# One core, LSH attention and a Mish feed-forward in one program: a new table of order and engine, and the bias of the exponential made by column

## The chip, the cores and the metric

The kernel runs on one core of a Trainium2 chip. The metric is the device time of one execution in microseconds. TensorE (PE) multiplies matrices, VectorE (DVE), ScalarE (ACT) and GpSimd (POOL) work on elements, and SyncE (SP) issues the DMAs.

## The reference, cut to what matters

```python
# q, k, v: (4, 8, 768, 64) float32;  proj: (64, 6);  w_in: (512, 2048);  w_out: (2048, 512)
q_bits = (einsum('bhsd,dk->bhsk', q, proj) > 0)      # 6 hash bits a token
k_bits = (einsum('bhsd,dk->bhsk', k, proj) > 0)
mask   = bucket(q_bits)[..., :, None] == bucket(k_bits)[..., None, :]
scores = where(mask, q @ k^T / 8, -1e9)
scores = scores - max(scores)
attn   = exp(scores) / (sum(exp(scores)) + 1e-9)
x      = (attn @ v), heads side by side              # (3072, 512)
h      = x @ w_in
out    = (h * tanh(softplus(h))) @ w_out             # (3072, 512)
```

The inputs are float32. The matmuls of the kernel run in float16, with every operand split into a high part and a rest.

## The kernel before, in words

The rows are worked through in 12 units of 256 tokens. A unit has 8 attention steps, each with the scores of two heads for 128 tokens, and 8 feed-forward steps, each with 256 columns of the inner width. Step numbers run through the program: S0 to S95 are the score matmuls (line 802), V0 to V47 the products with v (line 882, one for two score steps), H0 to H95 the first matmul of the feed-forward (lines 913 to 915), and O the second (lines 951 to 953, two for each H).

One attention step goes like this. PE fills `ps_s`, which exists once and holds the scores of both heads, with S. DVE takes the negated maximum of each head (line 809), makes from it a factor (line 812: the scale where the maximum is that of a real key, else 0) and a bias (line 815: maximum times factor); all of them lie in the small tile `svb`, one column for a head. ACT does the exponential of each head with this bias and factor (line 825) into `pb`, and sums it. Only then may the next S overwrite `ps_s`. The sums are inverted (lines 838, 841, 847). The attention is split into float16 parts in `hl`: the high part ("hi") on POOL, ACT or DVE (lines 365, 367, 368), the rest ("lo") in one instruction of DVE (line 386) or in two of POOL (lines 392 and 393). SP then transposes `hl` into `PT` by DMA (line 427), and V reads that. The lines 809 to 815 have two forms: one that treats the two heads' columns in one instruction (128x2), and one that takes each column by itself (128x1, twice).

In a feed-forward step ACT does Mish on the accumulators (line 931) and DVE, ACT and POOL split the result for O. Mish and the exponential need different tables of ACT, so an `ACT_TABLE_LOAD` stands wherever the one follows the other.

At the start the program also loads k, v, q and the weights, splits the weights (16 pieces, up to about step S16), and for the first keys and values makes the rests on PE (line 414). Keys and queries are transposed by DMA (`KT`, `QT`), hashed on PE (line 666), and the hash bits of both are written by DVE (line 674) and transposed as well; S0 needs all four.

What runs where, and in which order, is no decision of the code at run time. Every step of the program is an entry with one to four alternatives (an engine, a cost, a function). `ORDER` is a table of 2639 numbers, each with a letter for the alternative; the program issues the entries in the table's order, and each engine works through its own part in that order. SP issues all DMAs from one queue.

Of the kernel before, what the change touches and what calls it, by code (L numbers as in the profile page):

```python
# [92 lines left out]
151b 143 244b 141c 146c 317 76 144 147 152 153 159 107c 145 148 191c 184 160 183 108 149 218 245c 192 171 172
219 193 164b 194b 199 200 228 195 268b 201 227 162 226 202 173b 165 203b 185 197 204 211 174b 161 205 229 246
207b 212b 196 175 230 247 213 186 214 187 206b 220 296 231c 221 209 163 386 198 269b 208 232 222 239 240b 223
254 233 270b 235 92 189 255 234 241 210 236 224 242 256c 237 264 225 271 257 258c 238 272 297 265b 298b 260b 273
259b 274 281 176 266 188 276 267 280 262 284c 279 299 282 300 261 292 275 283 285 322b 263 248 287 277 348 286b
293b 249 288 333 294 290 190 295 289 349 307 309c 310 334 311 308 250b 350c 318 251b 312 335 319b 291 301 320
313b 252 302 351 321 304c 315 344 352 373b 303c 253 323b 336b 337 314 360 338 324 345 353 346 325 359 316 340
326 347 374 341 339c 354 305 327 375b 413 361b 328 362 306 342 376 356 369 398 355c 414 357 329b 343 363 330c  # L100
399 278 415b 370b 377 331 365b 400 364c 372 378 367 371 379 416 385 387 384 409 453b 381 401b 366 402 368 435
425 434 403b 388 404b 436 446 332 410b 454b 424 417 389b 380b 405 455c 412 411 391 382 456 447 479c 407 358 448
426b 449 406 427 480b 418 419 392 429b 408 393 450b 462 394 457 421 463 428b 383 430 420b 481b 422 432 451 482
437 431 458 390b 452 475 423 464b 483 459 514 433 465 489 466 460b 438 476 468 515 442 477 395 478 467c 469 396
439 516c 470 490c 517 507 443 599 488 491 440 508 509 492c 493 510 494b 484 485 499 518 444b 511b 486b 519 520
441 496 487 526c 397 461 445 512 527b 513 471 521b 535c 503 472 500 536 495 501 497 504 528b 547 523 548 537 473
522 505b 596 597 529 502 530 592 598 531 498 524 474 538 539 525 532 506 544 533c 550 534 540 551b 541 552 553c
549 561b 574c 554 582 560 600 555 556 601 557 575 543 588 558c 576 559 562 565c 566 542 602 563b 567b 564 568
569 578 577c 570 619 545 620 571 585 603 604c 589 615 572c 605 580 621 643 622 606c 623 579 573 581 616b 624
608b 593 714 546 625c 644 617 584 647 651 618 627 586 626b 658 628 587 583 594c 654 590c 634 591 652 609 595 645  # L110
689 612 635 607 653 715 716 718 636 659 688 610b 655b 660 613 661 656 638 629 662c 646 664 630 637 614 642 632
657 648 717 842 671c 631 611 639 665 640b 633 672 649b 684 673 679 674 685 650 675 719 677 663c 680 686 720c 687
703 722 641 690 681 666 704 726 667 691 692 682 705b 669 668 676 693 711 707b 738 727b 730 706 678 694b 729 696
670 697 739 741 728 753 712 721 742 709 723 695c 740 757 752 758 710 743b 731 734 732 759 760 754b 744 724c 708
698 745b 751 735 755 699 761 725 747 762 763c 780 756 765 772 746 788 773 700 733 701 749 736 748 783 766 781
774 791 789 784b 775 785 776 782 702 838 792 737 806 786 750 777 807 802 790 778 793c 794 892 803 795 787 834
833 804 797 805 846 825d 826 796c 779 835 764c 808 799 809 767 839 840b 850 800 768 810 827b 851 847b 821 836
837 854 811 845 769 812b 822 770 855 844 829 801 871 843 823 798 848 858 841 849 771 814 863c 873 828b 852c 813
853 859 864 872 815 831 865 867b 860 874b 893 816 817 886 894 895 713 1112 819 832 905 875 896c 876 830 877c 885
898 856b 888 866 868 899 818 857 878 820 906 869b 887 879 861b 889b 881 880b 907 890 891 870 908 919 911 1023  # L120
912 900 883b 922 913b 882 901 923b 915 941 914c 924 917 683 925 1068 909 926 884 927 942 897b 920 943 937 945
938 946 862 928 947 939 934 953 916 935b 918 949 930 944 948 970 929b 940 960b 1069 1111 968 931 954 961 932b
971 950 962b 903 1070 1071 824 964 963 933 951 972 973 969 983 966 982 957 952 965 985 974 955 975 976b 986 902
978 967 984 987 989 977c 979 1113 988 958 993 1015 956 1002 1001 904 994 1019 995c 980b 1016 1003 996c 959 1072b
1074 1028 1020 997 990 1004 1005 1017 999 1073c 1006b 1230 991 981 1075 1007 1021 1018 1260 1008b 1024 1025 1010
998 936 1026 1014 992 1048 1009c 1027 1012 1032 1022 1029 1049 1033 1039d 1040 1047 1061 1000 1041b 1030 1050b
1076 1043 1232 1034c 1051 1052 1011 1077 1013 1042b 1231 1062 1036 1031 1045 1053d 1054 1037 1233 1064 1035 910b
1038 1044 1063 921 1234 1055 1093 1065 1235 1081 1066 1082 1057 1067 1046 1056c 1085b 1083 1086 1059b 1087c 1084
1058 1096 1097 1098 1089 1088b 1099 1108 1094 1114 1100 1101 1118 1060 1115 1090 1078 1200 1102c 1119 1091 1122
1103 1123 1120c 1104 1106 1116b 1124 1125 1092 1137b 1117 1134 1135 1126 1138 1109 1121 1130 1147 1139b 1136  # L130
1145 1141b 1107 1148b 1105 1127 1131 1146 1079 1140b 1159 1149 1095 1132 1133 1150 1128c 1151b 1152 1129 1192
1142 1162 1193 1196 1153 1163b 1143b 1154b 1161 1157 1236b 1155 1194c 1293 1197 1080 1144 1178 1164 1165 1167
1170c 1179 1171 1168 1156 1160 1195 1224 1172 1205 1173b 1237 1180 1198b 1174 1181 1238 1182 1176b 1158 1201
1183b 1184 1185b 1166 1202b 1209 1169 1187b 1213 1203 1204 1199 1226 1216c 1175 1253 1177 1186b 1214 1206 1191
1217 1218c 1188 1189b 1227 1239 1207c 1292 1220 1210 1228 1225 1215 1190 1229 1208 1219 1254 1211c 1273 1240
1221 1212 1256 1245d 1241 1246 1261 1222 1110 1255 1247b 1257 1249 1258 1223 1259 1315 1248b 1274 1275 1251 1276
1277d 1288 1278 1279 1281b 1289b 1290 1262 1322 1263 1316b 1291 1318 1250 1326 1323 1285 1243 1280b 1319 1252
1320b 1264c 1282 1283 1307d 1308 1242 1324 1327 1330 1309 1321 1266 1328 1334 1331 1286b 1311 1310b 1313 1335
1338 1351 1332c 1284 1244 1325 1329 1353 1333 1343c 1339 1442 1267 1352 1312 1265 1294 1336 1344 1345b 1340 1381
1268 1354 1347 1387 1269 1295 1346b 1355 1337 1314 1356 1296 1380 1383 1297 1341c 1271 1349 1492 1287 1298b  # L140
1372d 1373 1348 1270 1350 1433 1374b 1384 1375 1376 1385 1386 1272 1382 1388 1378 1389 1377 1342 1300 1393c 1402
1358 1394 1395 1403 1299 1397 1391 1404 1434 1357 1301 1405 1438 1390 1396b 1446 1435 1392 1379 1439 1359 1302
1398 1450 1399 1360 1303 1425 1304 1305 1440b 1426 1427b 1306 1361 1447 1362 1451 1363b 1454 1436 1452b 1428c
# [950 lines left out]
```

## Time and profile before

| | before |
|---|---|
| median of 3 runs | 876.47 us (876.2 to 877.28) |
| profiled execution, span | 876.5 us |
| PE busy | 803.2 us (92%) |
| DVE busy | 695.7 us (79%) |
| ACT busy | 597.0 us (68%) |
| POOL busy | 280.6 us (32%) |
| ACT table loads | 74 |

The profiled execution's span, from the first to the last instruction, is its device time here; it equals the median of the runs. In the page, "busy" of an engine is the time in which it executes; a busy digit in the 40 slices is the tenth of a slice. PE's work comes in a fixed amount, so the time is PE's busy time and the time in which PE has nothing to do.

### The profile page before, as it was taken

How to read it: one execution, taken by the hardware profiler on the slowest of the kernel's cores; microseconds unless marked ns; L12 is line 12 of the kernel's file. 1: busy time of each engine (PE TensorE's matmuls, PEld its weight loads, DVE VectorE, ACT ScalarE, POOL GpSimd, SP SyncE). 2: the span in 40 equal slices, each digit the busy share in tenths (PEclk: the TensorE clock that was granted, in tenths of full speed). 3: DMA queues.
4: the chain of work that ended last, by engine and by line, in shares of the span. 5: the costliest groups of instructions: out<-in, count | busy, mean ns of one | idle time of the engine just before them, and what ended most of it. 6: DMA issues, size and time to landing. Idle time of an engine off the chain costs nothing.

```text
span 876.5 us, 17009 instructions
## 1 busy us (share of the span) xinstructions
PE 803.2 (92%) x6530; PEld 536.5 (61%) x6530; DVE 695.7 (79%) x1344; ACT 597.0 (68%) x947; POOL 280.6 (32%) x260
## 2 busy tenths in 40 slices
PE   2676679899999999999999999999999999999998
PEld 1343347566666767666656766666665766776665
DVE  4697999999899887788889879879888777676412
ACT  5587889878786667668777766567876756657411
POOL 4226443134146433443223212133413143351000
PEclk9697999999999999999999999999999999999999
DMA  9999989589999797688999966899997866556400
GB/s 279 268 243 235 215 195 224 155 187 196 200 172 173 146 186 123 132 156 169 211 188 192 175 122 117 150 178 182 230 161 143 154 120 129 101 98 128 78 25 25
DMA packets 432689, 143.73 MB, mean 164 GB/s; under 512 B 402912, under 2 KB 423392, under 8 KB 432608
## 3 DMA queue, kind: packets, MB, share of 16 engines
q1 hardware_dynamic: 432608, 142.65, 80.9%
q8 instruction: 51, 0.84, 0.4%
q14 instruction: 30, 0.25, 0.1%
HBM read 35.65 MB, written 6.29 MB: 48 GB/s over the span
## 4 chain that ended last, share of the span: by engine, by line
PE 58%; DVE 23%; DMA 8%; ACT 6%; issue 4%; SPq 1%; ACTq 0%; DVEq 0%
PE ps_s L802 10%; PE ps_t L882 8%; DVE svb L809 7%; PE ps_acc L913 7%; PE ps_o L951 6%; PE ps_acc L915 6%; PE ps_acc L914 6%; PE ps_o L953 6%; PE ps_o L952 6%; ACT pb L825 3%; DMA QT<-tok 3%; DVE hl L386 3%; DVE svb L812 1%; DVE ffb L386 1%; DVE svb L815 1%
## 5 line engine op out<-in xcount | busy, mean ns | idle before, releaser
L825 ACT ACTIVATE pb<-ps_s,svb 128x768 f32<-128x768 f32 x192 | 188.8, 986 | 100.9 <-DVE svb L815 84.5
L913 PE MATMUL ps_acc<-X,wi 128*128 128x256 f16 x768 | 209.8, 273 | 0.5 <-ACT ffb L931 0.5
L914 PE MATMUL ps_acc<-X,wi 128*128 128x256 f16 x768 | 209.6, 273 | 0.0
L915 PE MATMUL ps_acc<-X,wi 128*128 128x256 f16 x768 | 209.6, 273 | 0.0
L809 DVE TENSOR_REDUCE svb<-ps_s 128x2 f32<-128x1536 f32 x96 | 168.3, 1753 | 40.6 <-PE ps_s L802 39.4
L386 DVE SCALAR_TENSOR_TENSOR hl<-pb,svb,hl 128x768 f16<-128x768 f32 x146 | 155.8, 1075 | 3.3 <-POOL hl L365 2.7
L802 PE MATMUL ps_s<-KT,QT 128*128 128x512 f16 (+1 forms) x768 | 146.1, 335 | 10.3 <-ACT pb L825 9.7
L953 PE MATMUL ps_o<-wo,ffb 128*128 128x512 f16 x384 | 145.7, 379 | 0.3 <-DVE ffb L386 0.3
L951 PE MATMUL ps_o<-wo,ffb 128*128 128x512 f16 x384 | 145.7, 379 | 0.0
L952 PE MATMUL ps_o<-wo,ffb 128*128 128x512 f16 x384 | 145.7, 379 | 0.0
L365 POOL TENSOR_SCALAR hl<-pb,svb 128x768 f16<-128x768 f32 x66 | 65.3, 990 | 169.8 <-DVE svb L847 73.2
L882 PE MATMUL ps_t<-PT,VT 128*64 128x256 f16 x1728 | 107.6, 280 | 10.9 <-DVE hw L456 4.2
L802 PEld LDWEIGHTS <-QT 128*128 128x128 f16 x768 | 74.2, 99 | 67.2 <-issue 24.1
L882 PEld LDWEIGHTS <-VT 128*64 128x64 f16 x1728 | 94.5, 113 | 29.4 <-issue 23.8
L931 ACT ACTIVATE ffb<-ps_acc,smalls 128x512 f32<-128x512 f32 x96 | 63.5, 684 | 56.0 <-PE ps_acc L915 51.6
L367 ACT ACTIVATE hl<-pb,svb 128x768 f16<-128x768 f32 x77 | 70.9, 929 | 34.1 <-DMA PT<-hl 17.2
L386 DVE SCALAR_TENSOR_TENSOR ffb<-ffb,smalls 128x512 f16<-128x512 f32 x96 | 77.1, 813 | 14.5 <-POOL ffb L365 10.9
L392 POOL TENSOR_SCALAR pb<-pb,svb 128x768 f32<-128x768 f32 x42 | 44.6, 1062 | 136.0 <-ACT hl L367 40.3
L914 PEld LDWEIGHTS <-wi 128*128 128x128 f16 x768 | 75.2, 98 | 14.3 <-issue 1.1
L913 PEld LDWEIGHTS <-wi 128*128 128x128 f16 x768 | 75.1, 98 | 13.1 <-issue 1.4
L915 PEld LDWEIGHTS <-wi 128*128 128x128 f16 x768 | 75.1, 98 | 8.9
L393 POOL TENSOR_TENSOR hl<-pb,hl 128x768 f16<-128x768 f32 x42 | 70.8, 1686 | 3.5
(172 smaller groups left out, 1015.9 us busy)
## 6 DMA issues: line engine op xcount, KB each, us to landing
out_dram<-ffb SPq DMA_DIRECT2D x24, 256.0 KB, 2.8
stg<-in_k_dram SPq DMA_DIRECT2D x12, 384.0 KB, 4.1
stg<-in_v_dram SPq DMA_DIRECT2D x12, 384.0 KB, 4.1
stg<-in_q_dram SPq DMA_DIRECT2D x9, 512.0 KB, 4.9
wi<-in_moe_w_in_dram SPq DMA_DIRECT2D x7, 512.0 KB, 4.9
wo<-in_moe_w_in_dram SPq DMA_DIRECT2D x6, 512.0 KB, 5.1
stg<-in_moe_w_out_dram SPq DMA_DIRECT2D x6, 512.0 KB, 4.7
PT<-hl SPq DMA_TRANSPOSE x192, 4.0
```

The costliest lines, as they stand in the source:

```text
L367: ACT=lambda: nc.scalar.activation(dst, src, AF.Copy, scale=sc),
L386: return [("DVE", 215 + 1.035 * n, port(lambda: nc.vector.scalar_tensor_tensor(out=dst, in0=src, scalar=sc, in1=hi, op0=ALU.mult, op1=ALU. ...
L802: nc.tensor.matmul(ps_s[:, hh * S + c0 * P:hh * S + c1 * P], QTb[:, u % 2, sl, qi], KTb[:, j, sl, hh * NCH + c0:hh * NCH + c1].rearrange(" ...
L809: nc.vector.tensor_reduce(out=sv[:, 0], in_=ps_s.rearrange("p (h e) -> p h e", h=2), axis=AX.X, op=ALU.max, negate=True)
L825: EXP[n, hh] = op("exp", [("ACT", 1075, lambda hh=hh, t=t: nc.scalar.activation(pb[:, t], ps_s[:, hh * S:(hh + 1) * S], AF.Exp, bias=sv[:, ...
L882: nc.tensor.matmul(pv[hh * D:(hh + 1) * D, 0:256], vt[:, w, hh * NCH + c], pt[:, hh, a * NCH + c].rearrange("p s t -> p (s t)"), start=(x ...
L913: nc.tensor.matmul(o, wh, X[:, 0, c], start=(c == 0), stop=False)
L914: nc.tensor.matmul(o, wh, X[:, 1, c], start=False, stop=False)
L915: nc.tensor.matmul(o, wl, X[:, 0, c], start=False, stop=(c == NCC - 1))
L951: nc.tensor.matmul(PS[f"o{s}"], gh, wo[:, g, 0, f2], start=first, stop=False)
L952: nc.tensor.matmul(PS[f"o{s}"], gh, wo[:, g, 1, f2], start=False, stop=False)
L953: nc.tensor.matmul(PS[f"o{s}"], gl, wo[:, g, 0, f2], start=False, stop=last)
```

## The change

The code of `scale` is edited in its one-column form, and the table is exchanged as a whole. The one-column form had one product of two tensors for each column; now it is a product with a scalar for each partition, the factor of that column. The two-column form computes what it did. The second entry of "max" has 2305 in place of 2300 as its cost, which no code reads at run time.

```diff
 ORDER = """
-12 6 3 13 1 7 2 8 51 17 61 0 4 77 33 9 20 52 62 14 10 21 18 19 53 15 49 22 65 24c 97 26 5 16 23 63 34b 46 36c
...
+1 0 2 154 3 13 4 12 7 6 14 5 33 52 77 51 53 54 20 15 16 8 17 9 10 21 18 19 24c 22 23 34c 61 36c 26 37 62 46b 35b 27
...
-            for w in (slice(0, 1), slice(1, 2)) if single else (slice(0, 2),):
-                nc.vector.tensor_tensor(out=sv[:, 2, w], in0=sv[:, 0, w], in1=sv[:, 1, w], op=ALU.mult)
-        op("max", [("DVE", 2200, lambda: scale(False)), ("DVE", 2300, lambda: scale(True))],
+            if single:
+                for w in (slice(0, 1), slice(1, 2)):
+                    nc.vector.tensor_scalar(out=sv[:, 2, w], in0=sv[:, 0, w], scalar1=sv[:, 1, w], scalar2=None,
+                                            op0=ALU.mult)
+            else:
+                nc.vector.tensor_tensor(out=sv[:, 2], in0=sv[:, 0], in1=sv[:, 1], op=ALU.mult)
+        op("max", [("DVE", 2200, lambda: scale(False)), ("DVE", 2305, lambda: scale(True))],
```

What the two tables give to the engines, counted in the programs as built (rows whose count differs by much; the rest of the 2639 entries keep their engine):

| entry | before | after |
|---|---|---|
| attention rest, DVE / POOL | 146 / 42 | 173 / 15 |
| attention high part, DVE / ACT / POOL | 49 / 77 / 66 | 74 / 81 / 37 |
| feed-forward high part, DVE / ACT / POOL | 35 / 27 / 34 | 31 / 36 / 29 |
| bias by column, instructions | 98 products of two tensors | 98 products with a scalar |
| ACT table loads | 74 | 92 |

The numbers of steps and of instructions on PE stay the same; their order differs almost everywhere. At S20, PE has two O steps less behind it than before.

The lines of the changed program are five lower above `scale`, and lower by five to one behind it: line 802 is now 797, 809 is 804, 812 is 807, 825 is 824, 386 is 381, 427 is 422.

Three places show how the order moves. The first is SP's queue at the start: `wi`, `PT`, `stg` and `X` are tiles that the loads fill, `tok_64` and `wo` hold the high part and rest of the first queries and keys, `tok_65` the hash bits of the queries. Before:

```order
L423 DMA wi<-in_k_dram 128x2x384
L423 DMA wi<-in_v_dram 128x2x384 x2
L423 DMA PT<-in_k_dram 128x2x384
L423 DMA stg<-in_moe_w_in_dram 128x2x512
L423 DMA X<-in_q_dram 128x8x128
L423 DMA stg<-in_moe_w_in_dram 128x2x512
L423 DMA PT<-in_k_dram 128x2x384
L423 DMA PT<-in_v_dram 128x2x384 x2
L427 DMA_TRANSPOSE QT<-tok_64 128x16x128
L427 DMA_TRANSPOSE KT<-wo 128x12x128 x2
L427 DMA_TRANSPOSE QT<-tok_65 128x16x128
L427 DMA_TRANSPOSE KT<-wo 128x12x128
```

After, in the same place:

```order
L418 DMA wi<-in_v_dram 128x2x384 x2
L418 DMA wi<-in_k_dram 128x2x384
L418 DMA PT<-in_k_dram 128x2x384
L418 DMA PT<-in_v_dram 128x2x384
L418 DMA stg<-in_moe_w_in_dram 128x2x512 x2
L422 DMA_TRANSPOSE QT<-tok_64 128x16x128
L422 DMA_TRANSPOSE KT<-wo 128x12x128 x2
L422 DMA_TRANSPOSE QT<-tok_65 128x16x128
L422 DMA_TRANSPOSE KT<-wo 128x12x128
L418 DMA PT<-in_k_dram 128x2x384
L418 DMA wo<-in_moe_w_in_dram 128x2x512 x2
L418 DMA PT<-in_v_dram 128x2x384
```

One load of q (into `X`), one of k and one of v (into `PT`) have moved from ahead of the first transposes to behind them.

The second place is DVE from the maximum of S33 on, where both tables have the one-column form. Before:

```order
L809 TENSOR_REDUCE svb<-ps_s 128x2
L812 TENSOR_SCALAR svb<-svb,smalls 128x1 x2
L815 TENSOR_TENSOR svb<-svb 128x1 x2
L386 SCALAR_TENSOR_TENSOR hl<-pb,svb,hl 128x768
L368 TENSOR_SCALAR ffb<-ffb,smalls 128x512
L670 TENSOR_REDUCE hsum<-ps_t 128x96
L386 SCALAR_TENSOR_TENSOR ffb<-ffb,smalls 128x512
L386 SCALAR_TENSOR_TENSOR hl<-pb,svb,hl 128x768
L847 RECIPROCAL svb<-svb 128x2
```

After:

```order
L804 TENSOR_REDUCE svb<-ps_s 128x2
L807 TENSOR_SCALAR svb<-svb,smalls 128x1 x2
L811 TENSOR_SCALAR svb<-svb 128x1 x2
L363 TENSOR_SCALAR ffb<-ffb,smalls 128x512
L363 TENSOR_SCALAR hl<-pb,svb 128x768
L381 SCALAR_TENSOR_TENSOR ffb<-ffb,smalls 128x512
L381 SCALAR_TENSOR_TENSOR hl<-pb,svb,hl 128x768
L451 TENSOR_SCALAR smalls<-ps_t 128x2
L435 TENSOR_SCALAR smalls<-smalls 128x2
L846 RECIPROCAL svb<-svb 128x2
```

The two products are now of the TENSOR_SCALAR kind, and a high part (`hl<-pb,svb`) that another engine made stands on DVE.

The third place is ACT from the exponentials of S59 on (`pb,svb<-ps_s,svb`; the next such rows are S60's), with the Mish steps (`ffb<-ps_acc`). Before:

```order
L825 ACTIVATE pb,svb<-ps_s,svb 128x768 x2
L931 ACT_TABLE_LOAD
L931 ACTIVATE ffb<-ps_acc_1078,smalls 128x512
L931 ACTIVATE ffb<-ps_acc_1079,smalls 128x512
L838 ACTIVATE svb<-svb 128x2
L367 ACTIVATE tok_64<-stg,smalls 128x12x64
L825 ACT_TABLE_LOAD
L825 ACTIVATE pb,svb<-ps_s,svb 128x768
L931 ACT_TABLE_LOAD
L931 ACTIVATE ffb<-ps_acc_1078,smalls 128x512
L931 ACTIVATE ffb<-ps_acc_1079,smalls 128x512
L825 ACT_TABLE_LOAD
```

After:

```order
L824 ACTIVATE pb,svb<-ps_s,svb 128x768 x2
L362 ACTIVATE ffb<-ffb,smalls 128x512
L362 ACTIVATE tok_64<-stg,smalls 128x12x64
L930 ACT_TABLE_LOAD
L930 ACTIVATE ffb<-ps_acc_1062,smalls 128x512
L930 ACTIVATE ffb<-ps_acc_1063,smalls 128x512
L824 ACT_TABLE_LOAD
L824 ACTIVATE pb,svb<-ps_s,svb 128x768 x2
L362 ACTIVATE hl<-pb,svb 128x768
L887 ACTIVATE X<-ps_t,smalls 128x256
L362 ACTIVATE ffb<-ffb,smalls 128x512 x2
```

Two Mish steps stood ahead of the first head of S60 and two more between its two heads, each pair with a table load to either side; now one pair stands ahead of S60, and its two heads follow each other.

More of the change, by code (lines that the diff above doesn't have):

```diff
@@ L93 @@
[L93 to L107, printed above, removed]
@@ new lines @@
+112 58 57 107c 56 98 59 60 108b 93 69 94 99c 95 100 96 166c 101 167 122c 48 134 88 168b 123 84 126c 86 130c 135b
+124b 215b 127 70 120 121 113 90 49 125c 169 131 136 216 137 73 102 128 138d 139 103 140 132b 129 114 150 170 115
+217c 71 177 72 116b 104 133 151 155 142b 164 117b 143 178 156c 152 157 74 118 153 141c 158 75 165 179 105 146c 199
+191c 92 144 91 192 218 119 145 180 181 268 193 147 200 106 182b 243 159 148 160 195 171 201 149 76 202 184 196 219
+203b 211 183c 172 162 194 185 204 173 212 228 205 244b 174b 227 197 175 229 230 198 213 207 206c 214 226 186 209
@@ new lines @@
+1403 1379 1438 1336b 1395 1316b 1404 1396b 1361 1382 1305 1397 1352 1442 1362 1398 1405 1399 1363b 1381 1443 1425
+1426 1304 1427c 1306 1439 1365b 1446 1287 1450 1447b 1428 1406 1366 1436c 1448 1458 1429 1400 1364c 1431 1407 1454
+1449 1430 1459 1463b 1408 1460 1432 1337 1440c 1367 1451 1473 1368 1464 1437 1465b 1387 1474 1409 1401 1466 1421
+1370 1467 1410 1455 1433 1411 1468 1476 1412 1422 1472 1423 1414 1506 1456c 1475 1415 1369 1469 1441 1371 1488 1507
+1477 1445 1478 1452 1508 1479 1471 1470 1489 1416 1537 1481 1490 1480c 1482 1509b 1417 1483 1485 1491 1413c 1484
@@ new lines @@
+1453 1493 1522 1418 1419 1511b 1512 1712 1420 1513c 1494 1487 1523 1317 1541 1515 1524 1495 1516 1525 1496c 1486
+1498 1514 1545 1538 1497c 1499 1526 1444 1517 1505 1527 1546 1668 1542 1528 1549 1518 1529c 1547 1543c 1530 1500
+1553 1623 1424 1531 1501 1539b 1457 1548 1510 1830 1669 1540 1570 1532 1670 1534 1560d 1671 1533 1461 1561 1571
+1672b 1519 1535 1562 1569 1462 1572 1564 1557 1563 1573 1566 1585 1565 1558 1550 1559 1574b 1575 1590 1586b 1567
+1554 1551 1520 1831 1576b 1615 1591 1544 1587 1555c 1578 1568 1674 1579 1588 1583 1503 1502 1577 1552 1504 1592 1602
@@ new lines @@
+2076 1887 2001 1917 1968 2075 2021 1969 2010 2072 2011 2012c 1970 2014 2022 2088 2077 2023 2015 2078 2041 2080 2106
+2089 2079b 2055 1971 2071 2070 2045 2107 2053 2090 2108 2086 2083 2081 2016 2141 2017 2013b 2082 2091 2109c 2093
+2019 2111b 2084 2018 2112 2113c 2122 2115 2094 2137 2116 2123b 2114b 2020 2056 2095 2124 2085 2096c 2098 2125 2105
+2142 2223 2057 2099 2145 2044 2126b 2024 2117 2268 2138 2087 2061c 2127 2143 2146 2149 2139 2128b 2130 2153 2150
+2140 2131 2148 2151 2118 2100 2119 2147 2097 2170 2120b 2154 2160b 2101 2161 2134 2171b 2163b 2162b 2269 2168 2129
@@ new lines @@
+2103 2164 2270 2219 2102 2132 2173 2271 2133 2166 2157 2062 2172 2121 2174c 2175 2152 2185 2165 2158 2144 2135 2312
+2220 2176b 2169 2104 2186b 2272 2183 2232 2178 2187 2159 2179 2274 2190 2188 2177c 2167 2180b 2193 2194 2202 2196
+2189 2203b 2181 2195 2182 2275 2197 2204 2215 2199 2205 2200 2191 2206 2207 2155c 2224 2156 2216 2192 2198 2273c
+2184 2225b 2217 2228 2208c 2226 2210 2221c 2276 2211 2218 2214 2209 2222 2248 2277 2227 2110 2229 2212 2249 2213
+2201 2239c 2233 2240 2250b 2241b 2230b 2236 2242c 2251 2234c 2262 2231 2243 2247 2311 2244 2252 2313 2245 2261 2237
@@ new lines @@
+2380b 2371 2372c 2381 2409 2374 2395 2375 2382 2373c 2383 2401 2384 2376 2410 2377 2366 2402 2406 2391 2369 2403
+2361 2385c 2387 2413 2399 2388 2404 2407c 2386c 2389 2426 2414 2416d 2390 2417 2415 2425 2427 2378 2418c 2428 2439
+2420 2419c 2446 2421 2429 2411b 2430d 2431 2432 2412 2441 2408 2422 2424 2442 2434b 2423 2445 2438 2435 2444 2472
+2443 2440 2447 2448 2460 2433c 2449b 2436 2479 2450 2461 2437 2451 2295 2453 2475 2462 2452c 2454 2463 2483 2476
+2495 2484 2477b 2480 2491 2496 2464 2478 2465 2455 2466c 2485 2481c 2457 2467c 2468 2487 2473b 2469 2486 2470 2498c
```

176 lines of the change are left out of this document (78 added, 98 removed).

## The prediction

> **What bounds the kernel now.** I read the page's totals and slices first, then the busy time by stage, then the chain of waits at the start, the groups, and last the waits of PE.
>
> ```profile
> PE 803.2 (92%) x6530; PEld 536.5 (61%) x6530; DVE 695.7 (79%) x1344; ACT 597.0 (68%) x947; POOL 280.6 (32%) x260
> ...
> PE   2676679899999999999999999999999999999998
> ...
> DVE  4697999999899887788889879879888777676412
> ```
>
> PE works 803.2 of 876.5 us and is full from the tenth slice on; before that DVE is the fuller one. The table by stage says how much there is to win where. I cut it at DVE's maxima of S0, S8 and S20 and at the start of S95.
>
> ```profile
> core 0: us, PE busy (x) PEld busy (x) DVE busy (x) ACT busy (x) POOL busy (x), PEclk, DMA share, GB/s
> 0.00:31.50 31.50, 11.82 (x70) 6.28 (x70) 15.95 (x41) 16.25 (x30) 8.99 (x14) 0.84 1.00 268
> 31.50:94.00 62.50, 44.68 (x277) 25.66 (x277) 52.54 (x112) 48.57 (x83) 25.96 (x23) 0.84 1.05 240
> 94.00:209.70 115.70, 95.49 (x720) 60.90 (x719) 111.36 (x226) 98.60 (x150) 41.67 (x33) 0.96 0.87 197
> 209.70:369.00 159.30, 157.59 (x1345) 108.36 (x1343) 135.83 (x256) 112.48 (x177) 62.16 (x58) 1.00 0.86 165
> 369.00:520.00 151.00, 147.77 (x1283) 99.97 (x1282) 129.72 (x250) 110.31 (x178) 47.63 (x45) 1.00 0.94 174
> 520.00:660.00 140.00, 136.39 (x1178) 94.52 (x1177) 117.46 (x225) 97.40 (x157) 38.31 (x38) 1.00 0.89 168
> 660.00:808.70 148.70, 145.49 (x1174) 97.73 (x1172) 111.31 (x205) 95.48 (x150) 52.74 (x49) 1.00 0.67 124
> 808.70:876.50 67.80, 64.01 (x495) 43.07 (x493) 21.52 (x35) 17.90 (x26) 3.17 (x4) 1.00 0.20 46
> ```
>
> PE idles 19.7, 17.8 and 20.2 us in the first three stages (57.7 together). In the four stages from 209.7 to 808.7 it is busy 587.2 of 599.0 us, which leaves 11.8. The last stage idles 3.8 us, most of it the last output's way out. Since PE's work is the same after the change, the long middle can give back at most 11.8 us, and the start is where a new order can win or lose most. From S8 to S20 DVE works 111.36 of 115.70 us (96%): there the time is DVE's work. From S0 to S8 it has 10.0 us of idle time. Before S0 nothing is full but the DMA engines (share 1.00).
>
> **The change part by part.** *The loads at the start.* The chain of waits begins with the DMA:
>
> ```profile
> 7.35 4.82 DMA stg<-in_moe_w_in_dram
> 12.17 8.18 DMA QT<-tok
> 20.35 4.30 DMA KT<-wo
> ```
>
> Sizes, and the time from issue to landing, stand with the DMA issues:
>
> ```profile
> PT<-hl SPq DMA_TRANSPOSE x192, 4.0
> stg<-in_k_dram SPq DMA_DIRECT2D x12, 384.0 KB, 4.1
> stg<-in_q_dram SPq DMA_DIRECT2D x9, 512.0 KB, 4.9
> ```
>
> The first transpose of the queries took 8.18 us from its issue, where the median transpose takes 4.0 us: it stands behind the loads. The new queue has one load of q and one each of k and v less ahead of it, 512 + 2 x 384 = 1280 KB, 4.8 us at the stage's 268 GB/s. At most the transpose's excess of 4.2 us goes. Against that, DVE now makes the high part of the first keys and a diagonal ahead of the rest of the queries, so the transpose is issued about 1 us later. I take S0 2 us earlier, between 4 us earlier and 1 us later. The three loads then land later, beside the first attention steps, where the DMA share is 1.05; their users are the second to fourth pairs of heads. That is part of the upper end.
>
> *Work moved between engines.* The groups that carry it, with the one-column products:
>
> ```profile
> L386 DVE SCALAR_TENSOR_TENSOR hl<-pb,svb,hl 128x768 f16<-128x768 f32 x146 | 155.8, 1075 | 3.3 <-POOL hl L365 2.7
> L368 DVE TENSOR_SCALAR hl<-pb,svb 128x768 f16<-128x768 f32 x49 | 34.2, 697 | 3.6 <-DMA PT<-hl 2.9
> L392 POOL TENSOR_SCALAR pb<-pb,svb 128x768 f32<-128x768 f32 x42 | 44.6, 1062 | 136.0 <-ACT hl L367 40.3 <-DVE hl L368 32.4 <-ACT ffb L931 22.6
> L393 POOL TENSOR_TENSOR hl<-pb,hl 128x768 f16<-128x768 f32 x42 | 70.8, 1686 | 3.5
> L815 DVE TENSOR_TENSOR svb<-svb 128x1 f32<-128x1 f32 x98 | 26.1, 296 | 0.0
> L812 DVE TENSOR_SCALAR svb<-svb,smalls 128x1 f32<-128x1 f32 x98 | 16.4, 209 | 1.7
> L841 DVE TENSOR_SCALAR svb<-svb 128x1 f32<-128x1 f32 x60 | 7.3, 147 | 16.4 <-ACT pb L825 16.4
> L931 ACT ACT_TABLE_LOAD x37 | 47.5, 1283 | 1.9 <-DVE ffb L386 1.3
> L825 ACT ACT_TABLE_LOAD x36 | 46.2, 1283 | 20.9 <-DVE svb L815 19.5 <-DVE svb L847 1.0
> ```
>
> The product with a per-partition scalar does not occur on `svb` before. Its nearest rows are 209 ns (line 812, a product of the same shape with a scalar for each partition) and 147 ns (line 841, immediates alone); above, the old product's 296 ns. I take 209: it has the same kind of operand. So 98 x (296 - 209) = 8.5 us of DVE's work goes, between 0 and 14.6. Of the moves, 27 rests add 27 x 1.075 = 29.0 us to DVE and 25 high parts 25 x 0.697 = 17.4 us, and POOL loses 27 rests at 1.062 + 1.686 = 2.7 us each. In all DVE gets about 36 us more, nearly all of it after S20.
>
> By stage, each instruction at its group's mean: between S0 and S8 DVE gets 9.1 us more (two rests 2.2, four high parts 2.8, the rest weights and keys that come earlier); between S8 and S20 5.2 us less (five rests +5.4; three high parts -2.1; one-column products, 14 before and 12 after, -1.6; weights and feed-forward pieces done earlier or by others -6.9). The ends of DVE's instructions overlap, its busy time being about 0.91 of the sum of durations, so this is +8.3 and -4.7 us. What the first does to the time depends on the idle 10.0 us of that stage:
>
> ```profile
> DVE svb L809 <- PE ps_s L802: 4.2, 3, 2.5
> DVE hl L368 <- DMA PT<-hl: 2.2, 1, 2.2
> ```
>
> Work fills such waits only where it is ready and stands ahead of the waiting instruction. I take half of the idle time as filled: +3.3 us, between 0 (all but 1.7 us refilled) and +8.3 (none). From S8 to S20 DVE is full, so -4.7 counts whole; if weights are then waited for, nothing of it counts.
>
> *Less of POOL beside DVE.* In S8 to S20, six POOL rests become one.
>
> ```profile
> 507.28 1.02 DVE L386 SCALAR_TENSOR_TENSOR hl<-pb,svb,hl 128x768 f16<-128x768 f32 x1
> ```
>
> DVE's rest took 1.02 us here, with POOL not working, and 1.075 us on the mean of all. Some twenty-five of them in the stage and a like share of the other DVE work, 0.055 / 1.075 = 5% of half of it, give about 2 us. Bounds: 0 and 4.
>
> *The order on PE.* At S20 PE has two O steps less behind it. An O is six matmuls, and its rhythm is seen in the first and last of 24 matmuls:
>
> ```profile
> 512.37 0.38 PE L951 MATMUL ps_o<-wo,ffb 128*128 128x512 f16 x1
> ...
> 517.33 0.38 PE L953 MATMUL ps_o<-wo,ffb 128*128 128x512 f16 x1
> ```
>
> (517.33 - 512.37) / 23 = 0.216 us, an O 1.3 us. What is not done by S20 is done later by a full PE: +2.6 us.
>
> *The middle.* The next S waits until both exponentials have read the scores. With a table load ahead, that looks so (S57, no wait in it but its own chain):
>
> ```profile
> 503.64 1.46 PE L802 MATMUL ps_s<-KT,QT 128*128 128x512 f16 x8
> 505.14 1.76 DVE L809 TENSOR_REDUCE svb<-ps_s 128x2 f32<-128x1536 f32 x1 [1.38 <-PE ps_s L802]
> 507.46 1.28 ACT L825 ACT_TABLE_LOAD   x1 [1.53 <-DVE svb L815]
> 509.74 0.98 ACT L825 ACTIVATE pb<-ps_s,svb 128x768 f32<-128x768 f32 x1
> 511.06 1.47 PE L802 MATMUL ps_s<-KT,QT 128*128 128x512 f16 x8
> ```
>
> The waits of PE in the middle put a price on it (us in total, times, longest):
>
> ```profile
> PE ps_s L802 <- ACT pb L825: 4.0, 9, 1.1
> ```
>
> From the end of S57 (505.10) to the end of the second exponential (510.72) are 5.6 us, 4.3 without the load; PE has other work of 6.0 us in between. PE's waits for the exponentials are 4.0 us in the whole middle. By the two orders, priced at PE's rhythm (an O 1.3 us, the others alike from their starts), the steps from S20 on with a load ahead rise from 28 to 41, and those of them with less than 6.7 us of other work from 5 to 13; none has less than 6.0. Steps without a load and less than 5 us fall from 9 to 5. Eighteen more loads cost ACT 23 us, hidden by an ACT that is idle 30% of the middle; the cover is gone where DVE starts the maximum late by over 0.4 us. I price the eight new close places at 0.3 us each, +2.4. The shorter bias (0.17 us a step) and the fewer close places without a load give back up to the 4.0 us; I take 2.4. Net 0, between -4 and +10. DVE's 36 us more lie under a PE that is busy 98%.
>
> The Trainium skill (ScalarE: Activation LUTs, What ACT_TABLE_LOAD costs) puts a switch of tables at 1283 ns and another 1380 ns of drain, 2.66 us in all. The trace agrees with the first figure and not with the second, since the exponential starts 1.29 us after the load did. By the page's figure the chain would be 7.0 us, and an estimate from it would put the close places near 10 us more; I leave it out of the sum.
>
> **The sum.** -2.0 + 3.3 - 4.7 - 2.0 + 2.6 + 0 = -2.8 us against the profiled execution's 876.5, that is 873.7 us. The execution equals the median of the runs.
>
> **The rivals.** *Slower: PE waits for the exponentials.* With 41 loads ahead of exponentials and a DVE that holds one more 1.0 us rest in many steps, the maximum comes late. If it is late by 1.0 us in the 13 close places, each costs 1.0 - 0.4 = 0.6 us or 8 us, and the start stays as it was: 884. It decides from 0.4 us of lateness on. For it: DVE has to take 36 us more. Against it: DVE is at most 86% busy in the middle stages.
>
> *Slower: the start.* S0 to S8 fills no idle time (+8.3), S8 to S20 as summed: +2.3 net of the other terms; 879.
>
> *No change.* DVE stays full up to S20 and its work there is nearly equal in both tables, so that the gains at S0 and POOL just pay for the two O steps: 876.
>
> *Much faster.* Regular steps and fewer of POOL's slow rests (2.7 us where DVE takes 1.1) halve the middle's 11.8 us of idle time, -6, and S0 to S8 takes its 8.3 us wholly into idle time: 867.
>
> *The scalar product brings nothing.* If it takes 296 ns as before, the sum of DVE is 8.5 us higher and the start 1 us later: 874.8, within the no-change case.
>
> **How the numbers follow.** Under 0.2% (1.75 us) this kernel's measurement cannot be told from no change; the runs before span 1.1 us. As summed, faster by 2 to 6 us: 0.32. Much faster: 0.15. No change: 0.21. Slower by the exponentials 0.22, by the start 0.10. Faster is 0.47, the same 0.21, slower 0.32. The range of 8 in 10 takes in the two far rivals, 865 to 884; the likeliest case alone is 870 to 874.7.
>
> **What would show it.** The maximum of S0 starts near 29.5 us instead of 31.5, and the first QT transpose takes under 6 us. S20's maximum comes near 204 us. The one-column product reads near 0.2 us, with no long ones. PE's waits for the exponentials stay near 4 us from S20 on, and its idle time there near 12. If S8 comes later than 98 us, the half of the idle time was wrong; if PE's idle time in the middle is over 18 us, the table loads have won.

## The result, and the profile after

The changed kernel takes 869.76 us in the median against 876.34 us of the kernel before beside it: a ratio of 0.9925, 95% interval 0.9901 to 0.9949, or 6.6 us less (4.5 to 8.7). One of its four runs was disturbed (1062.97 us) and is left out; with it the median is 870.39 us.

The two profiled executions differ by more, 876.5 us against 866.5. Both numbers are spans. Ahead of the prediction the span was taken for the device time, and it is not: in the runs that give both, the device time is 1.7 to 2.3 us above it. So the execution profiled before was about 2 us slower than its median, and the one after (868.58 us with its span of 866.5) about 1 us faster. Totals are therefore compared by the runs below, and the profiles by their stages; of the 10.0 us between the two profiles some 3 us belong to the two executions and not to the change.

The page of the kernel after:

```profile
PE 801.8 (93%) x6530; PEld 538.6 (62%) x6530; DVE 695.2 (80%) x1404; ACT 620.6 (72%) x964; POOL 167.3 (19%) x171
...
DVE  6889889999989898789889877898897967976421
ACT  5679899887868768877969777686768767566221
POOL 4322223213221111002111123002233030101000
```

DVE made 60 instructions more in the same busy time, 695 us; ACT works 24 us longer, POOL 113 us less. PE does what it did. The busy time by stage, cut at the same places as before (S0's maximum, S8's, S20's; the later cuts differ somewhat):

```profile
0.00:27.80 27.80, 11.09 (x70) 6.09 (x70) 15.98 (x36) 11.90 (x22) 13.03 (x17) 0.98 0.94 244
27.80:93.10 65.30, 44.32 (x287) 24.87 (x287) 59.15 (x127) 55.02 (x90) 15.94 (x16) 0.87 1.13 256
93.10:202.60 109.50, 92.74 (x694) 62.41 (x694) 102.03 (x216) 92.59 (x141) 26.87 (x24) 0.91 0.96 206
202.60:358.20 155.60, 154.21 (x1330) 106.87 (x1329) 136.44 (x271) 119.29 (x190) 29.12 (x30) 1.00 0.92 171
358.20:512.40 154.20, 150.25 (x1292) 100.86 (x1291) 128.56 (x264) 123.33 (x189) 25.76 (x27) 1.00 0.91 170
512.40:654.30 141.90, 141.06 (x1210) 97.48 (x1209) 119.68 (x244) 102.12 (x159) 30.67 (x34) 1.00 0.91 171
654.30:795.70 141.40, 141.03 (x1186) 97.45 (x1185) 110.47 (x211) 99.60 (x150) 24.02 (x24) 1.00 0.68 120
795.70:866.50 70.80, 67.06 (x472) 42.54 (x469) 22.84 (x39) 16.71 (x27) 1.86 (x2) 1.00 0.24 52
```

From S20 on PE's idle time in the four middle stages is 1.39 + 3.95 + 0.84 + 0.37 = 6.6 us, where it was 11.8. In the three stages before, it is 16.7, 21.0 and 16.8 us, where it was 19.7, 17.8 and 20.2. S8 to S20 takes 109.5 us in place of 115.7. The groups that the prediction priced, by form:

```profile
L381 DVE SCALAR_TENSOR_TENSOR hl<-pb,svb,hl 128x768 f16<-128x768 f32 x173 | 177.1, 1033 | 8.9 <-POOL hl L360 5.3 <-ACT hl L362 2.6
...
L824 ACT ACT_TABLE_LOAD x45 | 57.7, 1283 | 18.4 <-DVE svb L811 12.8 <-DVE svb L814 4.5 <-DVE hl L381 0.7
L363 DVE TENSOR_SCALAR hl<-pb,svb 128x768 f16<-128x768 f32 x74 | 45.5, 616 | 4.7 <-DMA PT<-hl 3.9
L811 DVE TENSOR_SCALAR svb<-svb 128x1 f32<-128x1 f32 x98 | 16.3, 208 | 0.0
```

The new product takes 208 ns (296 before), a rest 1033 ns (1075), a high part 616 ns (697).

That the rests and high parts got shorter too has one cause in the traces. Count the instructions of DVE that take more than a tenth plus 40 ns longer than the median of their own form. Before there are 95, and together they exceed their medians by 57.2 us. All 95 start while an instruction of POOL is at work, and each ends its usual length after a moment 0.13 to 0.22 us ahead of that instruction's end: POOL holds them. After there are 26, with 13.2 us. By stage the held time falls from 3.3 to 1.6 us between S0 and S8, from 10.1 to 1.8 between S8 and S20, and from 42.3 to 9.0 between S20 and S95. That is how DVE could take on more work in the same busy time.

The waits of PE from S20 to S95:

```profile
PE ps_s L797 <- ACT pb L824: 3.1, 5, 1.4
```

With 45 loads ahead of exponentials instead of 36, PE waits for them 5 times where it waited 9 times, 3.1 us where it was 4.0.

For the experiments the stages are cut a little differently, at the maximum of S95 as the last. The lengths in us, each from one profiled execution:

| | to S0 | S0 to S8 | S8 to S20 | S20 to S95 | rest |
|---|---|---|---|---|---|
| before | 31.5 | 62.5 | 115.7 | 600.5 | 66.3 |
| after | 27.8 | 65.3 | 109.5 | 594.6 | 69.3 |
| new product alone | 30.4 | 63.6 | 111.7 | 595.9 | 66.3 |
| new table alone | 27.4 | 65.1 | 109.0 | 595.9 | 69.3 |
| new product, issued twice | 31.1 | 62.7 | 116.9 | 601.0 | 66.3 |

The profiled execution of the new product alone also had a higher granted clock of PE in the first three stages (1.00, 0.89 and 0.98, where before it was 0.84, 0.84 and 0.96), so a part of its shorter S8 to S20 can be the clock.

### The profile page after: what moved, and what is told of

It is laid out like the page before. It is cut to its first block, busy times and chain, and to the rows that moved or that the text cites. A ratio compares the mean times of both kernels' runs of the same rounds, so it can differ in the third digit from the quotient of the medians.

```text
span 866.5 us, 16987 instructions
## 1 busy us (share of the span) xinstructions
PE 801.8 (93%) x6530; PEld 538.6 (62%) x6530; DVE 695.2 (80%) x1404; ACT 620.6 (72%) x964; POOL 167.3 (19%) x171
## 5 line engine op out<-in xcount | busy, mean ns | idle before, releaser
L381 DVE SCALAR_TENSOR_TENSOR hl<-pb,svb,hl 128x768 f16<-128x768 f32 x173 | 177.1, 1033 | 8.9 <-POOL hl L360 5.3
L881 PE MATMUL ps_t<-PT,VT 128*64 128x256 f16 x1728 | 110.5, 284 | 8.0 <-DMA PT<-hl 5.8
L881 PEld LDWEIGHTS <-VT 128*64 128x64 f16 x1728 | 96.7, 114 | 25.0 <-issue 16.9
L362 ACT ACTIVATE hl<-pb,svb 128x768 f16<-128x768 f32 x81 | 75.1, 930 | 28.0 <-DMA PT<-hl 15.8
L381 DVE SCALAR_TENSOR_TENSOR ffb<-ffb,smalls 128x512 f16<-128x512 f32 x96 | 72.0, 760 | 22.4 <-ACT ffb L362 18.1
L930 ACT ACTIVATE ffb<-ps_acc,smalls 128x512 f32<-128x512 f32 x96 | 63.6, 683 | 32.9 <-PE ps_acc L914 32.2
L952 PEld LDWEIGHTS <-ffb 128*128 128x128 f16 x384 | 37.5, 98 | 45.4
L360 POOL TENSOR_SCALAR hl<-pb,svb 128x768 f16<-128x768 f32 x37 | 36.1, 977 | 134.3 <-DMA PT<-hl 75.6
```

Source lines behind the costliest of these rows:

```text
L362: ACT=lambda: nc.scalar.activation(dst, src, AF.Copy, scale=sc),
L381: return [("DVE", 215 + 1.035 * n, port(lambda: nc.vector.scalar_tensor_tensor(out=dst, in0=src, scalar=sc, in1=hi, op0=ALU.mult, op1=ALU. ...
L881: nc.tensor.matmul(pv[hh * D:(hh + 1) * D, 0:256], vt[:, w, hh * NCH + c], pt[:, hh, a * NCH + c].rearrange("p s t -> p (s t)"), start=(x ...
L952: nc.tensor.matmul(PS[f"o{s}"], gl, wo[:, g, 0, f2], start=False, stop=last)
```

## The experiments

Each ratio is to the kernel before, run beside it on the same chip, with its 95% interval. Kernels are compared with each other by these ratios. Stage lengths and waits come from one profiled execution each, which lies mostly 1 to 2 us off its kernel's median.

**The two parts apart.** The new code with the old table, and the new table with the old code.

```diff
 ORDER = """
-1 0 2 154 3 13 4 12 7 6 14 5 33 52 77 51 53 54 20 15 16 8 17 9 10 21 18 19 24c 22 23 34c 61 36c 26 37 62 46b 35b 27
+12 6 3 13 1 7 2 8 51 17 61 0 4 77 33 9 20 52 62 14 10 21 18 19 53 15 49 22 65 24c 97 26 5 16 23 63 34b 46 36c
...
```

> The old table with the new one-column product. Of the changed kernel's gain (0.75%, 6.6 us) the theory of several terms gives this part 2 to 3 us: 98 products at 0.21 instead of 0.30 us, 13 of them before S20, where DVE is full. Expected 873 to 874.5 us. Rival 1, the product is the cause of most: 871 or less, since what goes is the long ones (up to 1.1 us) that hold up exponentials. Rival 2, DVE's small products lie beside other work everywhere: 876, no change.

Measured: 870.86 us, ratio 0.9932 (0.9908 to 0.9955). The other way round:

```diff
-                    nc.vector.tensor_scalar(out=sv[:, 2, w], in0=sv[:, 0, w], scalar1=sv[:, 1, w], scalar2=None,
-                                            op0=ALU.mult)
+                nc.vector.tensor_tensor(out=sv[:, 2, w], in0=sv[:, 0, w], in1=sv[:, 1, w], op=ALU.mult)
```

> The new table with the old product of two tensors. Several terms: 871.5 to 873.5 us, most of the gain stays with the table. Rival 1 (the product is the cause): 875 or more. Rival 2 (the product is hidden): 870, as the changed kernel. With only 167 us of POOL left beside DVE the products should also be shorter than the 296 ns they took before; expected 230 to 260 ns.

Measured: 870.52 us, ratio 0.9931 (0.9912 to 0.9951). So each part alone gives 0.7%, and both together 0.75%, clearly less than the sum. The tile view of the product shows what the code brings. Before, the product of two tensors (both forms):

```profile
L815 DVE TENSOR_TENSOR svb<-svb x145: 145/160/1116, 33.6 to 812.3; 128x1 f32<-128x1 f32 x98, 128x2 f32<-128x2 f32 x47
```

With the new product alone:

```profile
L810 DVE TENSOR_SCALAR svb<-svb x98: 203/207/215, 41.4 to 803.8; 128x1 f32<-128x1 f32 x98
```

The columns are the shortest, median and longest in ns. The old product is shorter by its median, 160 ns, but reaches 1116; the new one is always 203 to 215. Of the 98 old one-column products 28 were over 250 ns, 18.1 us in all. The same step, S43, shows why, in the timeline of the kernel before (start, length):

```profile
392.59 0.33 DVE L812 TENSOR_SCALAR svb<-svb,smalls 128x1 f32<-128x1 f32 x2
392.84 1.19 DVE L815 TENSOR_TENSOR svb<-svb 128x1 f32<-128x1 f32 x2
...
392.30 1.64 POOL L393 TENSOR_TENSOR hl<-pb,hl 128x768 f16<-128x768 f32 x1
...
394.07 0.99 ACT L825 ACTIVATE pb<-ps_s,svb 128x768 f32<-128x768 f32 x1 [2.86 <-DVE svb L815]
```

and of the new product with the old table:

```profile
387.38 0.33 DVE L806 TENSOR_SCALAR svb<-svb,smalls 128x1 f32<-128x1 f32 x2
387.63 0.33 DVE L810 TENSOR_SCALAR svb<-svb 128x1 f32<-128x1 f32 x2
...
387.20 1.64 POOL L387 TENSOR_TENSOR hl<-pb,hl 128x768 f16<-128x768 f32 x1
...
387.96 0.99 ACT L823 ACTIVATE pb<-ps_s,svb 128x768 f32<-128x768 f32 x1 [1.83 <-DVE svb L810]
```

The same instruction of POOL lies over the products in both. Before, they end when it ends (394.03 and 393.94) and the exponential starts 1.48 us after the first of DVE's small instructions; with the new product it starts after 0.58 us, while POOL still works until 388.84. All 28 long products start under a POOL instruction and end within 0.06 us of the end of one. Of the 70 short ones 40 start under none, 29 start only in its last 0.21 us (most of them the second column, behind a held first one), and one lies wholly under it. Of the new products 58 start under a POOL instruction, 51 of them lie wholly under it, and not one is longer for it. In the new table POOL works 167 us instead of 281, so there the old product is long 13 times instead of 28 (8.1 us).

From the maximum's end to the last product's end, the 49 one-column steps take 819 ns on the mean before (26 of them over 700), 620 with the new product (none), 674 with the new table alone (12). Shorter by 49 x 0.199 = 9.8 us, the time fell by 6.0.

The held time of all DVE instructions, 57.2 us before, is 44.0 with the new product alone, 18.2 with the new table alone and 13.2 with both. So both parts lift holds of POOL, and that the gains don't add fits this. It is argued and not shown that this is all that the table does: it also has S0 4 us earlier, its last stage 3 us longer, and 18 more table loads.

**The table in two halves.** The tables joined at S20, both with the new product: new up to S20 and old from there, and the reverse. The diff shows the first joint, against the new table: behind 704 stand the entries not yet issued, in the old table's order.

```diff
 892 650 678 717 703b 704
-726 705c 663c 667 707b 690 679 727b 691 711
+667 679 663c 720c 690 681 726 691 692 682
...
```

> The new table up to the score step S20, from there the entries that are left in the old table's order and with its engines; the new product throughout. If the start and the middle both carry the gain: S20's maximum near 202.6 us as in the changed kernel (209.7 before), then the old middle with PE idle for about 11 us: 871 to 873 us. Rival, all of the gain that stays is the middle's (what the start gains goes into the two O steps): 875 to 876.

> The old table up to S20, then the new one; the new product throughout. Both carry: S20 near 208 us, then PE idle for about 6.5 us in the middle: 869 to 871 us, since the two O steps are not owed here. Rival, the start carries all: 874 or more, with PE idle for 10 us and more in the middle.

Measured: 872.17 us (ratio 0.9954, 0.9938 to 0.9971) and 874.54 us (0.9976, 0.9961 to 0.999). The first is where both halves were to carry, and its interval overlaps that of the old table with the same product; the second is where the rival put it, and it is slower than either whole table. From S20 to S95 PE idles 10.3 and 13.2 us; in the second, 10.8 of them lie between S20 and S54, behind the joint. So the joint itself has a price, and these two runs don't tell what each half of a table is worth.

**Is it the quiet POOL that wins in the table?** In the old table all 42 rests of POOL go to DVE, in the old order; once with the old product, once with the new. In the table the letter goes from each of the 42 numbers.

```diff
 -207b
+207
...
-260b
+260
...
```

> The old table and the old product of two tensors, but all 42 attention rests of POOL (two instructions, 2.7 us) are made by DVE (one, 1.08 us): +45 us of work on DVE, -115 us on POOL. Theory (the old product is held by POOL's instructions, and the new table wins where POOL does less): of the 28 products over 0.25 us at most 8 stay, their mean falls from 296 to about 200 ns, PE's idle time from S20 to S95 falls from 11.8 to about 8, and the time is 871 to 874. Rival (the new table wins by its order, and a DVE with 45 us more is late with the maxima): the long products go as well, but the time is 876 or more. If the products stay long, something else than POOL holds them.

Measured: 879.63 us, ratio 1.0036 (1.0023 to 1.0048): slower. The long one-column products did fall, from 28 to 9, and the mean chain from maximum to product from 819 to 634 ns. But the 45 us of rests on DVE cost more than that brought: S8 to S20, where DVE has no room, takes 117.7 us instead of 115.7. So the theory was nearly right on the products (at most 8 were to stay long) and wrong on the time, which came as the rival said: POOL holds the products, but taking its work away is no gain by itself. DVE's busy time rose by only 8.3 us (695.7 to 704.0), since its held time fell from 57.2 to 26.1.

> The old table with all 42 POOL rests on DVE, as before (879.63 us with the old product, whose mean there was 196 ns), now with the new product (208 ns). Theory (the new product is worth something only where POOL holds the old one): no gain, 878 to 881. Rival (the product of a scalar is worth its 5.4 us in any table): 874 to 875.

Measured: 878.43 us, ratio 1.0023 (1.001 to 1.0037), 1.1 us less than with the old product, with intervals that overlap. The same edit that is worth 6.0 us in the old table is worth about 1 us here, where it shortens the chain by only 14 ns a step: the new product pays where POOL would have held the old one.

**What DVE's time ahead of the exponential costs.** The old table with the new product issued twice.

```diff
             if single:
                 for w in (slice(0, 1), slice(1, 2)):
-                    nc.vector.tensor_scalar(out=sv[:, 2, w], in0=sv[:, 0, w], scalar1=sv[:, 1, w], ...)
+                    for _ in range(2):
+                        nc.vector.tensor_scalar(out=sv[:, 2, w], in0=sv[:, 0, w], scalar1=sv[:, 1, w], ...)
```

> The old table with the new product issued twice for each column (the second writes the same value again): 196 products of about 208 ns, 36 us of busy time in place of the old product's 26. Theory (what the old product cost was its long ones of up to 1.1 us, and 0.2 us more in every step is hidden): 870.5 to 873, faster than before although the products take more of DVE in all. Rival (the mean price counts: DVE's time ahead of the exponentials is paid in full): 20 us more of DVE, a third of it paid, 877 or more.

Measured: 879.95 us, ratio 1.0043 (1.0028 to 1.0059), that is 1.11% or 9.7 us more than with the product issued once. The theory that only the long ones count fell. The chain grew from 620 to 1118 ns in 49 steps, 24.4 us, so 0.40 of it was paid. The run can't tell the chain from DVE's work as a whole, which the second product raises too (busy 686.3 to 703.3 us). The group, and PE's waits from S20 to S95:

```profile
L811 DVE TENSOR_SCALAR svb<-svb 128x1 f32<-128x1 f32 x196 | 37.2, 211 | 3.5
```

```profile
PE ps_s L796 <- ACT pb L824: 5.5, 9, 1.2
```

By the stage table it came back where the single product had won, S8 to S20 (+5.2) and S20 to S95 (+5.1), and not at one price. Up to S20, with DVE full from S8 on, 13 of the steps with 6.5 us of chain cost 5.0 us (S20's maximum at 210.7 instead of 205.7); behind it 36 steps with 17.9 us cost 5.1.

**The other way to a shorter chain.** In the changed kernel the 49 one-column steps take the two-column form: two instructions instead of four. In the table the letter goes from each of the 49 numbers.

```diff
-135b
+135
...
-240b
+240
...
```

> The changed kernel with the maximum's 49 one-column steps in the two-column form: two DVE instructions instead of four after the maximum (median 0.46 us from the maximum's end to the last product's end against 0.62, with the longest ones 0.52 on the mean). Theory (DVE's time between the maximum and the exponential is paid at about 0.4 of itself, as the product issued twice showed: 9.1 us for 49 times 0.5 us): 49 x 0.10 to 0.16 x 0.4 = 2 to 3 us less, 867.4 to 868.4. Rival (the two-column instructions, one of them of two tensors, are held by POOL where the one-column ones are not, and the gain is given back): 870 to 872.

Measured: 874.17 us, ratio 0.9976 (0.996 to 0.9991), some 4.5 us slower than the changed kernel. My theory fell, and the rival too was short of it. The tile view:

```profile
L804 DVE TENSOR_SCALAR svb<-svb,smalls x96: 228/228/1545, 29.4 to 802.6; 128x2 f32<-128x2 f32 x96
```

```profile
PE ps_s L794 <- ACT pb L821: 4.9, 8, 1.4
```

The median chain in these steps is 460 ns instead of 620, but 12 of the 49 are over 700 and the longest is 1776: with two columns the first instruction too is held by POOL. The mean is 643 ns. Fewer and shorter instructions bought nothing, and the long cases cost. The loss is larger than the mean explains (49 x 0.023 us, and 47 x 0.011 in the other steps), and its cause is open; the new table alone has 12 such chains as well, up to 1613 ns, and lost nothing to speak of. Which of the long chains hit a PE with no other work, and which don't, I did not follow up.

**The loads at the start alone.** The old table with the new product, and only the three loads (one of q, k and v) behind the first transposes, with the two squares on ACT that read them.

```diff
 ORDER = """
-53 15 49 22
+53 15 22
...
-55 109b 87c 69 38 88 78c 56 54
+109b 87c 38 88 78c 54
...
-42 179 43
+42 43
...
-44 58
+44 55 56 49 58
...
-70
+69 70
...
-180
+179 180
```

> The old table with the new product, and only the three loads (one each of q, k and v) moved behind the first transposes in SP's queue, with the two squares on ACT that read them. Theory (the first transposes wait behind the loads): S0's maximum starts at 28 instead of 30.4, S8 and S20 about 1 us earlier than with the new product alone (94.0 and 205.7), since DVE is full there and takes only a part; 869.5 to 870.5 against 870.9 for the new product alone. Rival (the start is given by DVE's and ACT's work ahead of S0): S0 within 0.5 us of 30.4. Second rival (the moved loads are late for the second to fourth pair of heads): S8 later than 95.5 and the time over 871.5.

Measured: 873.99 us, ratio 0.9972 (0.9952 to 0.9992), about 3.5 us slower than the new product alone, with intervals that barely overlap. SP's transposes in the timeline (the length is that of SP's issuing), first with the new product alone:

```profile
12.04 6.70 SPq L421 DMA_TRANSPOSE QT<-tok  x1
```

then with the loads moved:

```profile
11.42 3.13 SPq L421 DMA_TRANSPOSE QT<-tok  x1
```

and after:

```profile
12.36 2.03 SPq L422 DMA_TRANSPOSE QT<-tok  x1
```

The first transposes do stand behind the loads: SP's 6.7 us become 3.1 and 2.0, and from issue to landing 8.7 us become 5.1 and 4.7 at most. S0's maximum came at 29.1 instead of 30.4. But the time came as the second rival said. PE's waits between 27 and 100 us, with the loads moved:

```profile
PE ps_t L660 <- DMA KT<-wo: 7.9, 1, 7.9
```

and without:

```profile
PE ps_t L660 <- DMA KT<-wo: 3.9, 1, 3.9
```

PE waits 4 us longer for the keys of the next pairs, and S8's maximum comes at 96.8 instead of 94.0. The profiled execution is the slowest of this kernel's twelve, 6.8 us above their median, so how much of this a usual execution has isn't shown. The new table also has the three loads behind the first transposes, and rearranges DVE and ACT behind them; alone the move is a loss.

**What the table loads cost.** The changed kernel with a plain copy in the place of Mish, so that the exponential's table is never displaced: one load in place of 92. The output is not the reference's.

```diff
-        op("mish", [("ACT", 690, lambda: nc.scalar.activation(ffb[:, t], PS[psn], AF.Mish, scale=hs[:, g:g + 1]))],
+        op("mish", [("ACT", 690, lambda: nc.scalar.activation(ffb[:, t], PS[psn], AF.Copy, scale=hs[:, g:g + 1]))],
```

> The changed kernel with Mish left out: a plain copy with the same scale stands in its place, so that the exponential's table is loaded once and about 90 table loads of 1283 ns go (117 us of ACT); the output is therefore not the reference's. Theory (the loads are hidden, but for a few close places): PE's idle time from S20 to S95 falls from 6.6 us to about 4 at least, and the time is 867 to 870. Rival (the loads are what holds the exponentials): PE's idle time there falls under 2 us, the 16.8 us from S8 to S20 fall by 5 or more, and the time is under 862.

Measured: 866.39 us, ratio 0.9889 (0.9862 to 0.9917), 3.2 us less than the changed kernel, with intervals that overlap a little; near the theory, and far from the rival. The copy takes as long as Mish (682 and 683 ns), so the loads are all that goes. PE's waits from S20 to S95, in the fastest of the six runs:

```profile
PE ps_s L795 <- ACT pb L822: 0.9, 2, 0.7
```

PE's idle time there is 3.1 us after 6.6. So 91 loads of 1.28 us, 117 us of ACT, are worth some 3 us, on the mean 0.04 us each.

**Order or engine?** The two tables differ in the order and, for 459 entries, in the engine. Crossed, with the new product: the new order with the old engines, and the old order with the new engines. The diff is that of the first, against the new table.

```diff
-24c 22 23 34c 61 36c 26 37 62 46b 35b 27
+24c 22 23 34b 61 36c 26 37 62 46 35c 27
...
```

> New product, the new table's order, but every entry on the engine it has in the old table (459 entries differ). With the new product the new table as a whole is worth about 0.5 us (870.9 to 870.4). Theory (with a product that POOL does not hold, moving work from POOL to DVE only costs, about 6 us by the 7.6 us that 45 us of rests cost above, and the new order earns it back): 864 to 867. Rival (order and engines only work together): 871 or more, with PE's idle time from S20 to S95 over 8 us.

> New product, the old table's order, every entry on the engine it has in the new table. Theory (the moves to DVE cost about 6 us when the order does not make room for them): 875 to 878. Rival (it is the engines that win, not the order): 870 or less.

Measured: 939.84 us (ratio 1.0717, 1.07 to 1.0735) and 939.41 us (1.0724, 1.0706 to 1.0742). Both are 7% slower. The rival of the first was right by far more than it said, and of the second neither side was. PE's longest sums of waits from S20 to S95, the first cross:

```profile
PE ps_s L796 <- ACT pb L823: 24.2, 27, 1.9
PE ps_o L949 <- DVE ffb L958: 5.8, 2, 3.7
```

and the second:

```profile
PE ps_s L795 <- ACT pb L822: 18.3, 21, 1.8
```

In either the scores wait for the exponentials more than twenty times, where the changed kernel waits five times. By these two runs the table's order and its engines only work together, and neither has a price by itself. (The price of the rests that the first expectation works with is, by the runs with the new product, 8.0 us: 0.9932 against 1.0023.)

None of these kernels beats the changed one by more than the intervals leave open; the one that leaves out Mish comes nearest.

## Why the prediction was right, and where it was not

The direction was right, and 869.8 us lies in the range, 865 to 884, and just below the likeliest case (870 to 874.7). The gain of 6.6 us is over twice the 2.8 that the sum gave; that it fell inside is in part the width of the range. The lengths below are those of the two profiles, which differ by some 3 us more than the runs.

**The start, -2.0.** It was -3.7 (S0's maximum at 27.8, foretold 29.5), and by the way foretold: the first transpose landed 4.7 us after its issue instead of 8.7. In the other runs S0's maximum comes at 30.3 to 31.5 us with the old start, at 27.4 to 28.9 with the new one. The upper end, that the moved loads come late, was just as real: alone the move cost some 3.5 us. With the rest of the new table S8 is not late (93.1 us).

**S0 to S8, +3.3.** It was +2.8. DVE does 6.6 us more there (59.15 after 52.54) and its idle time falls from 10.0 to 6.2 us; the half that was chosen was close.

**S8 to S20, -4.7 and -2.0 for POOL.** Together -6.7, measured -6.2, but the two sizes were not right. DVE's busy time fell by 9.3 us (111.36 to 102.03), and its held time by 8.3, where "less of POOL beside DVE" had been put at 2.0 and at most 4. The prediction took DVE's instructions at their groups' means, in which the holds were hidden. The new product alone, without any move, takes 3.7 us of the held time and gives -4.0. That the sum came out is luck.

**The two O steps, +2.6.** PE's busy time from S20 to the end grew by 2.3 us (651.3 to 653.6), so the term stands. That the last stage grew by 3.0 us is something else: the table with the old start and the new rest owes no O at S20 and has a last stage of the same length, 69.5 us.

**The middle, 0.** This is the step that failed: it was -5.9, and PE's idle time went from 11.8 to 6.6 us, foretold near 12. What could be won was bounded by PE's direct waits for exponentials, 4.0 us, of which 2.4 were taken. These waits fell by only 0.9 us (4.0 to 3.1); the other 4.3 us of idle time went in single waits of up to 1.4 us for other things (transposes, hash sums, small scalars), which the sum had not priced. The product was priced by its mean, and its long ones were not looked at: 0.17 us a step was counted, near the 0.20 us by which the chain shrank on the mean, but in single steps it shrank by up to 0.85 us. The new product alone gave -4.6 us from S20 to S95, and 3.5 us less idle time of PE. And the 18 more table loads, priced at +2.4, come to 18 x 0.04 = 0.7 us by the kernel without them. How the holds on DVE turn into each of PE's small waits was not followed.

**DVE's 36 us more.** They were taken to lie under PE. They did not appear as busy time at all: from S20 to S95 DVE is busy 495.1 us before and 495.3 after, because its held time falls there by 33.3 us. Where the order makes no room, added work is paid: in the old order 45 us of rests cost 8.0 us (0.9932 against 1.0023 with the new product).

**The rivals.** The exponentials were not late. "The scalar product brings nothing" is refuted by its run alone, -6.0 us. "Much faster" had the size of the middle right (about half of the 11.8 us of idle time gone), and fewer slow pieces on POOL beside it; that these are the cause in the table is not shown, since taken away by themselves they bring a loss.

**The base.** The span was taken for the device time. The profiled execution before was about 2 us slower than the median, so its span equalled the median by chance. This hardly touches the forecast, but the stage lengths: the runs give -6.6 where the profiles give -10.0.

The Trainium skill (SBUF — State Buffer, SBUF: two separate sides) says that VectorE and GpSimd share one pair of ports as an exclusive lock for a whole instruction, taken by a VectorE instruction with two inputs from SBUF or one in a two-port mode. The trace agrees: two-tensor products wait up to 1.1 us for POOL's end, one-column products with a scalar never. By that sentence the long products could have been foretold from the change alone; the prediction looked at means and missed it.

## What to carry to other kernels

Look at the longest of an instruction beside its median, before its mean: 160 ns with a longest of 1116 says that something holds it, and the engine whose instruction ends at the same moment says what. Do so for every group of the engine, the large ones too: the 57 us of holds on DVE here were four times those on the product. On the chain that releases PE, a form that is a little slower and never held beat one that is faster on the median (620 against 460 ns). The gains of two changes that each lift holds did not add, so each should be timed alone; and of this table, which fixes order and engine together, no part could be priced apart.

## What was not expected of the hardware

Which small DVE instructions POOL holds goes by their form: 128x1 with a scalar for each partition, 58 started under a POOL instruction and all took 203 to 215 ns; 128x1 of two tensors, up to 1116 ns; 128x2 with a scalar, 228 ns alone and up to 1545 under POOL (in the two-column run 17 of the 26 that started under it were held). Of the 96 reciprocals of 128x2 before, 19 started under POOL, and all took 147 to 167 ns.

Small instructions of DVE ahead of an exponential, 24.4 us more in all, cost 9.7 us although DVE is idle a fifth of the time, most dearly where DVE is full; 91 table loads of 1.28 us on ACT cost some 3 us.
